# A memory-attention and expert kernel on one core: 368 steps of its hand-written order put in other places

## The chip, the cores and the metric

The kernel runs on one core of a Trainium2 chip. The metric is the device time of one execution in microseconds (us). The core has a matrix engine (PE), three engines that work along 128 partitions (DVE, ACT, POOL), and a queue engine (SP) that issues all of this kernel's transfers. The engines run side by side, each through its own instructions in order, and wait for one another by semaphores.

## The reference

```
a   = softmax(phi over the tokens)            # per batch and head: 576 tokens, 32 memories
k_m = a^T k;  v_m = a^T v                     # 32 x 64 each
att = softmax(q k_m^T / 8) v_m                # 8 batches, 8 heads, 576 tokens, 64
x   = att, heads side by side                 # 576 x 512 per batch
e   = argmax(x w_gate), kept from the token before where sigmoid(x w_local) >= 0.5
out = softmax(x w_gate)[e] * (relu(x w1[e]) w2[e])   # 8 experts, 512 -> 1024 -> 512
```

All values are 32-bit. The expert of a batch's first token is used for the whole batch; tokens that chose another are redone in a loop at the end.

## The kernel before

**Work of one batch.** The attention gives `at`, the 576 softmax rows against the memories, which are put in two terms, `ah` (ACT, L990) and `al` (POOL, L994). The product of the memories' values with `w1` (`pg`, L1220) gives `G`, again in two terms, `Gh` (ACT, L1233) and `Gl` (DVE, L1235). The hidden layer (`hidden`, L1251) multiplies these: six matmuls per group, results in a PSUM bank `ph`, and each `ph` is taken out by ACT (L1259) and DVE (L1260). Then `w2` is multiplied in two forms: `turned` (L1283 to L1285, 448 tokens) and `natural` (L1268 to L1270, 128 tokens), for which `w2` is cut into `w2h` (ACT, L1207) and `w2l` (POOL, L1208).

**What comes before that for each batch.** The tokens' maxima of `phi` (`colmax`, L699; for batch 1 a tree of four steps, `cm`, L719), their turning and spreading on PE (`pm` L736, `mc`, `pm2` L749, `cx` L758), the subtraction (`sub`, L763), the exponential (`exp`, L767), the sums over tokens (`asum`), the product with keys and values on PE (`pkv`, L794, with `sums`, L810), and the turned memories (`kvn`, `pT`, `kvT`). Then the queries are turned (`q`, `qT`), and the scores (`psc`, L925) are taken out of PSUM by DVE (`turn`, L938) and go through `mx`, `sub`, `exp`, `sum`, `inv`, `mul`, `at` (L955 to L986) in parts: `o` (one row block), `p` and `z` in batch 0, `a` and `z` in the later ones. The gate is `pl0` and `choice` (L1010, L1023 to L1025) for the first token, whose result SP reads to address `w1`, and the `g` steps for all tokens (`g pl` L1035, `g carry` L1104 to L1120, `g prob` L1127 to L1135, `g cols` L1153 to L1162).

**What sets the order.** All batches are interleaved by hand. `SCHEDULE` is a table: its line 0 runs before the first group of the first hidden layer, and line n behind the n-th piece that the generator `moe` yields. A batch yields 12 pieces of `hidden` (four of 256 tokens with two groups each, then eight of 320 tokens), 32 of `turned` and 8 of `natural`, 52 in all. So lines 1 to 52 stand beside batch 0's expert and carry mostly batch 1's attention and batch 2's keys. A step is written `2 exp 0`: batch, name. Each step appends its instructions to the engines' streams at that place, and an engine never overtakes.

**Other resources.** PSUM has three pools: `pa` (3 banks), `ph` (3), `po` (2); the table `BANKS` says which of them a step uses. All transfers are issued by SP in the order of the table, and each waits until the one eight places before it has landed. The steps `warm ...` are matmuls on zeros that are used by nobody (L694).

Of the kernel before, what the change touches and what calls it, by code (L numbers as in the profile page):

```python
# [39 lines left out]
}  # L40

SCHEDULE = """
0 warm f, 0 phi 0, 0 colmax 0, 0 phi 1, 0 colmax 1, 0 kv tile, 0 q0 tile, 0 v 0, 0 k 0, 1 kv tile, 0 at, 0 k 1, 0 warm f, 0 warm f, 0 warm b, 0 v 1, 0 pm, 0 mc, 0 pm2, 0 cx, 0 dsub 0, 0 gate constants, 0 warm f, 0 warm f, 0 warm f, 0 warm f, 0 exp 0, 0 pkv a, 0 dsub 1, 0 warm b, 0 asum 0, 0 q0 a, 0 exp 1, 0 asum 1, 0 sums, 0 rinv, 0 pkv b, 0 kvn, 0 o q, 0 pT, 0 warm b, 0 warm b, 0 q0 b, 0 gate loads, 0 q0 c, 0 kvT, 0 o psc, 0 o turn, 0 o mx, 0 o sub, 0 o exp, 0 o sum, 0 o inv, 0 o mul, 0 gate turn, 0 p q 0, 0 p q 1 0, 0 pgg, 0 o at, 0 ggt, 0 p q 1 1, 0 pl0, 0 choice, 1 phi, 0 q0 d, 1 cm 0, 1 cm 1, 1 warm k, 0 p psc, 0 p turn, 2 phi, 0 p mx, 0 p sub 0, 0 p exp 0, 0 p sub 1, 1 cm 2, 0 p exp 1, 0 p sum 0, 1 warm v, 0 p sum 1, 0 p inv, 0 p mul 1, 0 z q 0, 0 z q 1, 0 expert, 0 z q 2, 0 w1 0 a, 1 pm, 1 mc, 0 p mul 0, 0 p at 0, 0 p ah 0, 0 w1 1 a, 0 pg lo, 0 Gh lo 0, 0 z psc, 0 w2 0, 0 z turn, 1 warm u, 0 warm b, 0 p at 1, 0 z mx, 1 v, 0 p al 0, 0 pg hi, 0 p ah 1, 0 p al 1, 0 Gh lo 1, 0 Gl lo, 0 z sub, 0 G hi, 1 pm2, 1 cx, 0 pg 1 lo, 0 G 1 lo, 0 z exp, 0 z sum
1 sub 1, 0 pg 1 hi, 1 exp 1, 0 z inv, 0 z mul, 0 z at, 0 G 1 hi, 0 split 0, 1 k, 0 z ah, 1 dsub 0, 0 w2 1

0 z al, 1 exp 0, 1 asum, 0 g pl

0 split 1, 0 split 2, 0 split 3
0 g lt

2 colmax, 1 pkv 0, 1 pkv 1, 1 sums, 1 rinv, 1 q 0, 0 g L, 0 split 4
0 split 5, 0 split 6

0 split 7, 1 q 1
1 kvn, 2 pm, 2 mc, 1 a qT 0

1 z qT 0, 0 g fresh, 0 g kept  # L60

1 pT, 2 pm2

2 cx
1 kvT, 1 z qT 1, 2 sub 1, 2 sub 0, 1 a qT 1, 1 a psc, 1 pgg, 1 a turn
1 a mx, 1 a sub  # L70


1 a exp

1 a sum
2 exp 0
2 kv, 0 g carry, 0 g exp, 0 g prob, 1 a inv

# [3 lines left out]


1 ggt, 1 pl0, 2 q 0, 1 a ah, 1 a al, 2 q 1, 1 z psc, 1 choice, 2 pkv 0, 2 pkv 1, 2 sums, 0 gate 0, 1 z turn, 1 expert, 2 rinv, 1 w1 0, 1 w1 1

1 z mx
2 z qT 0, 1 z sub
2 z qT 1, 2 kvn, 2 pT, 1 pg 0, 1 w2 0, 0 gate 3, 1 z exp, 2 kvT, 0 gate 2, 1 z sum, 1 z inv, 1 z mul, 1 z at, 1 g pl, 1 g lt, 3 phi, 0 evict, 1 G 0, 2 a qT 0, 2 z psc, 1 pg 1, 1 G 1, 2 z turn, 1 split 0, 1 split 1
2 z mx
1 z ah, 1 z al, 1 split 2

0 g present, 1 w2 1
1 kv store

1 split 3, 1 split 4, 1 split 5, 3 colmax

1 split 6, 2 a qT 1, 1 split 7

1 g L  # L110

0 store, 2 a psc, 3 kv, 2 a turn, 2 pgg, 0 kv store, 3 pm, 2 a mx, 2 a sub

1 g fresh

2 a exp
1 at store

1 g kept, 2 z sub, 2 z exp, 1 g carry, 2 z sum, 2 ggt


3 q 0, 0 row store, 2 z inv, 2 z mul, 2 z at


2 a sum, 2 z ah, 2 a inv
# [6 lines left out]
3 mc
2 a at, 2 pl0, 2 choice, 2 g pl, 2 g lt, 3 pm2

3 cx


3 sub 0, 3 exp 0, 3 a qT 0, 2 a ah  # L140

1 g exp, 1 g prob
2 expert, 2 w1 0, 2 w1 1, 2 pg 0, 3 sub 1, 3 exp 1, 3 z qT 0, 3 z qT 1, 2 w2 0, 1 g cols, 1 gate 0, 1 evict, 1 gate 2, 2 a al, 3 asum, 3 pkv 0, 2 G 0, 3 pkv 1, 2 g L, 2 z al, 2 split 0, 3 sums, 3 rinv, 3 a qT 1, 2 pg 1, 1 gate 1, 2 G 1
# [2 lines left out]
2 split 1, 2 w2 1, 2 split 2  # L150
# [1511 lines left out]
```

## Time and profile before

| | |
|---|---|
| device time, median of 3 runs | 390.9 us (390.81 to 391.11) |
| the profiled execution's own time | 392.12 us |
| its span, first to last instruction | 390.3 us |
| mean granted clock of PE | 0.993 |
| busy: PE, DVE, ACT, POOL | 98%, 73%, 44%, 40% |
| DMA: bytes moved, share of the 16 engines | 82.55 MB, 70% |

The profiled execution took 392.12 us, of which 390.3 us lie between its first and last instruction and 1.8 us around them. It lies 1.2 us above the median of the runs. A busy share is a mean over the whole span; where an engine waits is seen only in the rows.

### The profile page before, as it was taken

Reading aid. Unit: us, or ns where it says so; the run is one execution under the profiler, and the core shown is the slowest. Engines: PE = TensorE matmul, PEld = TensorE weight load, DVE = VectorE, ACT = ScalarE, POOL = GpSimd, SP = SyncE. Lnnn points to the kernel's source line nnn. Section 1 sums busy time; section 2 is a strip of 40 time slices with the busy share of each in tenths; the row PEclk is TensorE's granted clock in tenths of the full one; section 3 lists DMA queues with packets and bytes.
Section 4 is the critical chain, followed back from the end, with each engine's and each line's share of the span. In section 5 each row is a group of like instructions: output and inputs, shape, how many; then the busy total and the mean of one; then the engine's idle time right before and its main releaser. Section 6 shows DMA issues by size and latency. Waiting matters only on the chain. (4 is left out here: it accounts for less than half of the span.)

```text
span 390.3 us, 10303 instructions
## 1 busy us (share of the span) xinstructions
PE 382.3 (98%) x4088; PEld 329.8 (84%) x4088; DVE 285.2 (73%) x700; ACT 170.6 (44%) x430; POOL 157.3 (40%) x166
## 2 busy tenths in 40 slices
...
GB/s 232 265 285 395 139 265 176 268 351 325 142 101 329 268 171 179 349 304 141 273 215 225 114 165 314 135 322 226 127 359 294 123 109 16 183 267 179 0 36 91
DMA packets 119947, 82.55 MB, mean 211 GB/s; under 512 B 69972, under 2 KB 95320, under 8 KB 119896
## 3 DMA queue, kind: packets, MB, share of 16 engines
...
q14 instruction: 18, 0.15, 0.1%
...
## 5 line engine op out<-in xcount | busy, mean ns | idle before, releaser
L1208 POOL TENSOR_TENSOR w2l<-raw,w2h 128x512 fp32r<-128x512 f32 x64 | 81.4, 1298 | 49.0 <-ACT w2h L1207 28.4
L1283 PE MATMUL po<-h,w2l 128*128 128x448 f32 (+1 forms) x256 | 93.3, 365 | 0.0
L1285 PE MATMUL po<-h,w2h 128*128 128x448 f32 (+1 forms) x256 | 91.8, 359 | 0.0
L1284 PE MATMUL po<-h,w2h 128*128 128x448 f32 (+1 forms) x256 | 91.8, 359 | 0.0
L1260 DVE SCALAR_TENSOR_TENSOR h<-ph,h 128x320 fp32r<-128x320 f32 (+1 forms) x96 | 52.0, 553 | 32.5 <-ACT h L1259 32.0
L1251 PE MATMUL ph<-ah,Gh 128*128 128x256 f32 (+1 forms) x256 | 73.8, 303 | 0.0
L1251 PE MATMUL ph<-ah,Gl 128*128 128x256 f32 (+1 forms) x256 | 72.2, 296 | 0.0
L1294 POOL TENSOR_TENSOR oT<-oT,gT 128x448 f32<-128x448 f32 (+1 forms) x32 | 29.1, 925 | 85.0 <-ACT gT L1160 40.7
L1259 ACT ACTIVATE h<-ph 128x320 fp32r<-128x320 f32 (+1 forms) x96 | 46.3, 489 | 29.5 <-PE ph L1251 29.3
L1251 PE MATMUL ph<-al,Gh 128*128 128x256 f32 (+1 forms) x256 | 54.9, 295 | 0.0
L1251 PEld LDWEIGHTS ph<-ah,Gh 128*128 128x128 f32 x256 | 48.2, 188 | 4.3 <-issue 1.2
L1283 PEld LDWEIGHTS po<-h,w2l 128*128 128x128 f32 x256 | 48.3, 189 | 4.1 <-issue 0.7
L1285 PEld LDWEIGHTS po<-h,w2h 128*128 128x128 f32 x256 | 48.1, 188 | 3.6
L1284 PEld LDWEIGHTS po<-h,w2h 128*128 128x128 f32 x256 | 48.1, 188 | 3.2
L1251 PEld LDWEIGHTS ph<-ah,Gl 128*128 128x128 f32 x256 | 48.3, 189 | 0.4 <-DVE Gl L1235 0.2
L994 POOL TENSOR_TENSOR al<-at,ah 128x576 fp32r<-128x576 f32 (+1 forms) x18 | 23.7, 1319 | 44.4 <-ACT ah L990 44.2
L1251 PEld LDWEIGHTS ph<-al,Gh 128*128 128x128 f32 x256 | 41.1, 188 | 0.0
L1207 ACT ACTIVATE w2h<-raw 128x512 fp32r<-128x512 f32 x64 | 37.1, 626 | 0.1
L763 POOL TENSOR_TENSOR phi_t<-phi_t,cx 128x384 f32<-128x384 f32 (+1 forms) x13 | 18.5, 1436 | 41.5 <-ACT cx L758 30.0
L965 ACT ACTIVATE sc<-sc 128x576 f32<-128x576 f32 (+2 forms) x18 | 11.3, 631 | 47.6 <-DVE sc L960 47.6
L1268 PE MATMUL po<-w2h,h 128*128 128x512 f32 (+1 forms) x80 | 29.7, 371 | 0.0
L1269 PE MATMUL po<-w2l,h 128*128 128x512 f32 (+1 forms) x80 | 29.5, 369 | 0.0
...
## 6 DMA issues: line engine op xcount, KB each, us to landing
...
```

Of the source, the lines that this page charges most:

```text
L994: (eng or nc.gpsimd).tensor_tensor(out=st.al[:, gs, ss], in0=st.at[:, gs, ss], in1=st.ah[:, gs, ss], op=ALU.subtract)
L1207: nc.scalar.activation(h, src, AF.Copy)
L1208: nc.gpsimd.tensor_tensor(out=l, in0=src, in1=h, op=ALU.subtract)
L1251: nc.tensor.matmul(pv[:, c - c0], lhsT=lt[:, g, cs], rhs=rt[:, g, s0 : s0 + n], start=(i == 0), stop=(i == 5),)
L1259: nc.scalar.activation(hi, pv, AF.Relu)
L1260: nc.vector.scalar_tensor_tensor(out=lo, in0=pv, scalar=0.0, in1=hi, op0=ALU.max, op1=ALU.subtract)
L1268: nc.tensor.matmul(po, lhsT=ht[:, c, 0, ts], rhs=hi, start=(c == 0), stop=False)
L1269: nc.tensor.matmul(po, lhsT=ht[:, c, 0, ts], rhs=lo, start=False, stop=False)
L1283: nc.tensor.matmul(po[:, 0:n], lhsT=lo, rhs=ht[:, c, 0, s1:], start=(c == 0), stop=False)
L1284: nc.tensor.matmul(po[:, 0:n], lhsT=hi, rhs=ht[:, c, 0, s1:], start=False, stop=False)
L1285: nc.tensor.matmul(po[:, 0:n], lhsT=hi, rhs=ht[:, c, 1, s1:], start=False, stop=(c == FC - 1))
L1294: nc.gpsimd.tensor_tensor(out=x, in0=x, in1=g, op=ALU.mult)
```

## The change

The first 105 lines of `SCHEDULE` (0 to 104) are written anew: the work is the same except for the matmuls on zeros, 368 steps stand in other places, and from line 105 on nothing changes. The three steps with 39, 24 and 8 small matmuls on zeros become one step with 8, `warm n`, used eight times, and there are more of the 512-column ones. For batch 0 the steps `z ah` and `z al` are cut in two. `fetch_q` makes its tile at whichever half is fetched first.

```diff
 SCHEDULE = """
...
-2 kv, 0 g carry, 0 g exp, 0 g prob, 1 a inv
...
-0 at store, 2 exp 1, 0 g cols, 0 gate 1, 1 a mul, 2 asum, 1 a at
...
-1 ggt, 1 pl0, 2 q 0, 1 a ah, 1 a al, 2 q 1, 1 z psc, 1 choice, 2 pkv 0, 2 pkv 1, 2 sums, 0 gate 0, 1 z turn, 1 expert, 2 rinv, 1 w1 0, 1 w1 1
...
+1 pl0, 0 g exp, 1 choice, 1 z mx, 1 expert, 0 g prob
...
+2 exp 0, 2 pkv 0, 2 z qT 1, 2 pkv 1, 1 z exp, 2 asum, 2 sums, 2 rinv, 1 z sum, 2 kvn, 1 w1 0, 1 w1 1, 1 pg 0, 1 pg 1, 1 z inv, 1 z mul, 1 z at, 2 pT, 1 G 0, 1 z ah, 0 gate 0, 1 z al, 1 G 1, 1 w2 0, 1 split 0, 0 gate 1, 0 gate 3
...
+3 phi, 2 z psc, 2 pgg, 1 split 3, 3 kv, 2 z turn, 0 gate 2, 0 store, 2 a psc, 2 a turn
...
     def fetch_q(st, hs):
-        if hs.start == 0:
+        if not hasattr(st, "qt"):
             st.qt = pin.tile([P, HG, NB, 32], F32, tag="q", name="q_t", bufs=1)
...
-        "idle": lambda st: [nc.sync.drain(), nc.sync.drain()],
-        "warm u": lambda st: warm(39, 32, False),
-        "warm k": lambda st: warm(24, 32, False),
-        "warm v": lambda st: warm(8, 32, False),
+        "idle": lambda st: [nc.sync.drain() for _ in range(3)],
+        "warm n": lambda st: warm(8, 32, False),
...
     for g in range(NG):
         STEPS[f"p ah {g}"] = lambda st, g=g: k_ah(st, 0, PB, each[g])
+        STEPS[f"z ah {g}"] = lambda st, g=g: k_ah(st, PB, NB, each[g])
+        STEPS[f"z al {g}"] = lambda st, g=g: k_al(st, PB, NB, gs=each[g])
```

The first removed line of the table above is old line 34, then 42 and 45; the added ones are new lines 38, 48 and 58.

PE before, at the end of line 0 and into the first hidden group (`raw` with a number is one half of `w1`'s columns, taken in two quarters; `ph<-ah,Gh` is the hidden layer):

```order
L694 MATMUL wp<-wz 128x512
L1220 MATMUL pg<-raw_461,kvT 32x256 x8
L749 MATMUL pm<-ident,mcw 128x128
L1220 MATMUL pg<-raw_473,kvT 32x256 x8
L1251 MATMUL ph<-ah,Gh 128x256
L1251 MATMUL ph<-ah,Gl 128x256
```

PE in the changed kernel, at the same place:

```order
L1220 MATMUL pg<-raw_518,kvT 32x256 x8
L1251 MATMUL ph<-ah,Gh 128x256
L1251 MATMUL ph<-ah,Gl 128x256
L1251 MATMUL ph<-ah,Gh 128x256
L1251 MATMUL ph<-ah,Gl 128x256
L1251 MATMUL ph<-al,Gh 128x256 x2
L1251 MATMUL ph<-ah,Gh 128x256
L1251 MATMUL ph<-ah,Gl 128x256
L1251 MATMUL ph<-ah,Gh 128x256
L1251 MATMUL ph<-ah,Gl 128x256
L1251 MATMUL ph<-al,Gh 128x256 x2
L1220 MATMUL pg<-raw_521,kvT 32x256 x8
```

The product with the third quarter of `w1`'s columns (`pg<-raw_473`, eight matmuls, the step `0 pg 1 lo`) stood ahead of the hidden layer; it now stands, as `pg<-raw_521`, behind the first two hidden groups. `pm2` (L749) has moved further forward, and two matmuls on zeros and batch 0's `z psc` stand ahead of the piece shown.

ACT before, beside batch 0's `turned` and `natural` (`phi_t` is batch 2's exponential, `gT` and `gt` batch 0's gate values, `kvn` batch 2's):

```order
L767 ACTIVATE phi_t<-phi_t 128x4x192
L1075 ACTIVATE ex<-ex 32x144
L1125 ACTIVATE pr<-rt 32x18
L767 ACTIVATE phi_t<-phi_t 128x4x96
L1160 ACTIVATE gT<-gs 32x14 x4
L1162 ACTIVATE gt<-gs 32x1 x4
L876 ACTIVATE ggt_113<-pgg 128x9 x2
L990 ACTIVATE ah<-at 128x2x288
L832 ACTIVATE kvn<-pkv,rinv 128x128 x2
```

ACT in the changed kernel:

```order
L1075 ACTIVATE ex<-ex 32x144
L1125 ACTIVATE pr<-rt 32x18
L767 ACTIVATE phi_t<-phi_t 128x4x96
L990 ACTIVATE ah<-at 128x2x288
L1160 ACTIVATE gT<-gs 32x14 x4
L1162 ACTIVATE gt<-gs 32x1 x4
L767 ACTIVATE phi_t<-phi_t 128x4x192
L965 ACTIVATE sc<-sc 128x576
L832 ACTIVATE kvn<-pkv,rinv 128x128 x2
```

The larger exponential of batch 2 (128x4x192) stood ahead of the gate's eight copies; it now stands behind them, and directly ahead of the work that `pkv` releases.

## Rows read from the trace of the kernel before

**Rows 1.** The page's head and its first part: span, busy us and share of PE.
```profile
span 390.3 us, 10303 instructions
PE 382.3 (98%) x4088; PEld 329.8 (84%) x4088; DVE 285.2 (73%) x700; ACT 170.6 (44%) x430; POOL 157.3 (40%) x166
```

**Rows 2.** Windows: us; busy PE, PEld, DVE, ACT, POOL; granted clock; DMA share; GB/s.
```profile
26.00:28.00 2.00, 2.00 (x66) 1.28 (x47) 1.97 (x7) 1.02 (x3) 0.23 (x1) 0.68 0.92 306
28.00:30.00 2.00, 2.00 (x26) 0.75 (x33) 2.00 (x5) 1.19 (x4) 1.35 (x2) 0.50 1.02 345
34.00:44.00 10.00, 10.00 (x229) 9.40 (x228) 7.96 (x15) 7.97 (x18) 8.92 (x9) 1.00 0.98 286
```

**Rows 3.** Timeline of PE: start, us, instruction, count, idle before and its releaser.
```profile
19.35 0.77 PE L694 MATMUL wp<-wz 128*128 128x32 bf16 x24
20.05 0.66 PE L925 MATMUL psc<-qT,kvT 64*32 64x256 f32 x16
...
20.94 1.97 PE L912 MATMUL pq<-ident,q 128*64 128x128 f32 x32
...
24.73 0.30 PE L736 MATMUL pm<-ident,cm 128*128 128x128 f32 x1 [1.46 <-DVE cm L719]
25.01 1.01 PE L1220 MATMUL pg<-raw,kvT 64*32 64x256 f32 x9
...
26.65 1.64 PE L694 MATMUL wp<-wz 128*128 128x32 bf16 x40
28.22 1.23 PE L1220 MATMUL pg<-raw,kvT 64*32 64x256 f32 x16
...
29.79 0.79 PE L1220 MATMUL pg<-raw,kvT 64*32 64x256 f32 x16
30.50 0.39 PE L1251 MATMUL ph<-ah,Gh 128*128 128x256 f32 x1
...
32.13 0.66 PE L1220 MATMUL pg<-raw,kvT 64*32 64x256 f32 x16
```

**Rows 4.** Timelines of ACT, DVE and SP's queue, 18 to 24 us.
```profile
18.60 0.25 ACT L876 ACTIVATE ggt<-pgg 128x9 f32<-128x9 f32 x2
19.09 0.63 ACT L914 ACTIVATE qT<-pq 128x512 f32<-128x512 f32 x1 [0.24 <-PE pq L912]
...
19.73 0.15 DVE L1024 FIND_INDEX8 ei<-m,pl 1x8 uint32<-1x8 f32 x1
...
20.70 0.69 DVE L719 TENSOR_TENSOR tree<-phi_t 128x512 f32<-128x512 f32 x1 [0.56 <-DMA phi_t<-in_phi_dram]
...
20.61 3.25 SPq L1185 DMA_DIRECT2D raw<-in_moe_w_dram  x4
```

**Rows 5.** Timeline of PE beside batch 0's turned and natural products.
```profile
56.50 0.71 PE L925 MATMUL psc<-qT,kvT 64*32 64x288 f32 x16
...
69.70 2.21 PE L794 MATMUL pkv<-kv_t,phi_t 64*32 64x128 f32 x143
```

**Rows 6.** Timeline of DVE, 57 to 68 us.
```profile
57.30 0.85 DVE L938 STREAM_TRANSPOSE sc<-psc 128x288 f32<-128x288 f32 x2 [2.53 <-PE pgg L866]
58.18 0.75 DVE L955 TENSOR_REDUCE mx<-sc 128x18 f32<-128x576 f32 x1
...
61.15 0.22 DVE L1104 STREAM_TRANSPOSE endt<-end 32x64 f32<-32x64 f32 x1
...
62.27 0.25 DVE L1127 TENSOR_REDUCE es<-ex 32x18 f32<-32x144 f32 x1
...
64.83 0.18 DVE L1153 SCALAR_TENSOR_TENSOR gs<-pr,rb 32x18 f32<-32x18 f32 x1
...
65.60 2.24 DVE L699 TENSOR_REDUCE asum<-phi_t 128x128 f32<-128x1152 f32 x1
```

**Rows 7.** Timeline of ACT, 60 to 67 us.
```profile
60.35 0.83 ACT L767 ACTIVATE phi_t<-phi_t 128x768 f32<-128x768 f32 x1
...
65.04 0.89 ACT L1160 ACTIVATE gT<-gs 32x14 f32<-32x14 f32 x4 [2.04 <-DVE gs L1153]
65.96 0.84 ACT L1162 ACTIVATE gt<-gs 32x1 f32<-32x1 f32 x4
```

More of the change, by code (lines that the diff above doesn't have):

```diff
@@ L42 @@
 SCHEDULE = """
-0 warm f, 0 phi 0, 0 colmax 0, 0 phi 1, 0 colmax 1, 0 kv tile, 0 q0 tile, 0 v 0, 0 k 0, 1 kv tile, 0 at, 0 k 1, 0 warm f, 0 warm f, 0 warm b, 0 v 1, 0 pm, 0 mc, 0 pm2, 0 cx, 0 dsub 0, 0 gate constants, 0 warm f, 0 warm f, 0 warm f, 0 warm f, 0 exp 0, 0 pkv a, 0 dsub 1, 0 warm b, 0 asum 0, 0 q0 a, 0 exp 1, 0 asum 1, 0 sums, 0 rinv, 0 pkv b, 0 kvn, 0 o q, 0 pT, 0 warm b, 0 warm b, 0 q0 b, 0 gate loads, 0 q0 c, 0 kvT, 0 o psc, 0 o turn, 0 o mx, 0 o sub, 0 o exp, 0 o sum, 0 o inv, 0 o mul, 0 gate turn, 0 p q 0, 0 p q 1 0, 0 pgg, 0 o at, 0 ggt, 0 p q 1 1, 0 pl0, 0 choice, 1 phi, 0 q0 d, 1 cm 0, 1 cm 1, 1 warm k, 0 p psc, 0 p turn, 2 phi, 0 p mx, 0 p sub 0, 0 p exp 0, 0 p sub 1, 1 cm 2, 0 p exp 1, 0 p sum 0, 1 warm v, 0 p sum 1, 0 p inv, 0 p mul 1, 0 z q 0, 0 z q 1, 0 expert, 0 z q 2, 0 w1 0 a, 1 pm, 1 mc, 0 p mul 0, 0 p at 0, 0 p ah 0, 0 w1 1 a, 0 pg lo, 0 Gh lo 0, 0 z psc, 0 w2 0, 0 z turn, 1 warm u, 0 warm b, 0 p at 1, 0 z mx, 1 v, 0 p al 0, 0 pg hi, 0 p ah 1, 0 p al 1, 0 Gh lo 1, 0 Gl lo, 0 z sub, 0 G hi, 1 pm2, 1 cx, 0 pg 1 lo, 0 G 1 lo, 0 z exp, 0 z sum
@@ L44 @@
[L44 to L76, printed above, removed]
-2 kv, 0 g carry, 0 g exp, 0 g prob, 1 a inv
@@ L85 @@
-0 at store, 2 exp 1, 0 g cols, 0 gate 1, 1 a mul, 2 asum, 1 a at
-1 ggt, 1 pl0, 2 q 0, 1 a ah, 1 a al, 2 q 1, 1 z psc, 1 choice, 2 pkv 0, 2 pkv 1, 2 sums, 0 gate 0, 1 z turn, 1 expert, 2 rinv, 1 w1 0, 1 w1 1
[L93 to L127, printed above, removed]
+0 warm f, 0 phi 0, 0 colmax 0, 0 phi 1, 0 colmax 1, 0 kv tile, 0 q0 tile, 0 v 0, 0 k 0, 1 kv tile, 0 at, 0 k 1, 0 warm f, 0 warm f, 0 warm b, 0 v 1, 0 pm, 0 mc, 0 pm2, 0 cx, 0 dsub 0, 0 gate constants, 0 warm f, 0 warm f, 0 warm f, 0 warm f, 0 exp 0, 0 pkv a, 0 dsub 1, 0 warm b, 0 asum 0, 0 q0 a, 0 exp 1, 0 asum 1, 0 sums, 0 rinv, 0 pkv b, 0 kvn, 0 o q, 0 pT, 0 warm b, 0 warm b, 0 q0 b, 0 gate loads, 0 kvT, 0 o psc, 0 o turn, 0 o mx, 0 o sub, 0 o exp, 0 o sum, 0 p q 1 0, 0 o inv, 0 o mul, 0 gate turn, 0 o at, 1 phi, 1 cm 0, 0 p q 0, 0 pgg, 1 cm 1, 0 q0 c, 0 p q 1 1, 0 q0 d, 0 warm n, 0 warm n, 0 ggt, 0 pl0, 0 choice, 1 cm 2, 0 warm n, 0 warm n, 0 p psc, 0 p turn, 0 p mx, 0 p sub 0, 0 p exp 0, 0 warm n, 0 warm n, 0 warm n, 0 warm n, 0 warm b, 0 warm b, 0 warm b, 0 warm b, 0 p sub 1, 0 p exp 1, 1 pm, 1 mc, 0 p sum 0, 0 p sum 1, 1 k, 0 z q 0, 0 z q 1, 0 z q 2, 0 expert, 1 pm2, 0 p inv, 0 p mul 0, 1 cx, 0 p mul 1, 0 p at 0, 0 p ah 0, 0 warm b, 0 p al 0, 0 p at 1, 0 p ah 1, 0 p al 1, 0 warm b, 0 warm b, 1 dsub 0, 0 warm b, 0 w1 0 a, 0 w1 1 a, 0 pg lo, 0 Gh lo 0, 0 Gh lo 1, 0 Gl lo, 0 warm b, 0 warm b, 1 v, 0 z psc, 0 z turn, 0 z mx, 0 pg hi, 0 G hi, 0 z sub, 1 exp 0
@@ new lines @@
+0 pg 1 lo, 0 G 1 lo, 0 z exp, 0 z sum
+0 pg 1 hi, 0 G 1 hi, 0 z inv, 0 z mul, 0 z at, 1 sub 1, 1 exp 1, 1 asum, 0 z ah 0, 2 phi, 2 colmax
+1 pkv 0, 1 pkv 1, 1 sums, 1 rinv, 0 z al 0, 0 z ah 1, 0 g pl, 0 z al 1, 0 w2 0, 0 split 0, 0 split 1, 0 split 2, 0 split 3, 2 pm
+0 w2 1, 0 split 4, 1 q 0
+1 q 1
+0 split 5, 0 split 6, 2 mc
+1 kvn
+0 at store
+0 split 7
+2 kv, 0 g lt, 0 g L, 0 g fresh
+1 a qT 0, 1 pT, 1 z qT 0
+1 kvT
+1 z qT 1
+1 a qT 1
+1 pgg, 1 ggt, 2 q 1, 0 g kept, 0 g carry, 1 a psc, 1 a turn, 1 a mx, 1 a sub, 1 z psc, 2 pm2, 2 cx
@@ new lines @@
+1 a exp, 1 a sum, 1 a inv, 1 a mul, 1 a at
+2 sub 0
+1 z turn
+1 pl0, 0 g exp, 1 choice, 1 z mx, 1 expert, 0 g prob
+2 sub 1, 2 exp 1
+1 a ah, 1 z sub, 0 g cols
+1 a al
+2 exp 0, 2 pkv 0, 2 z qT 1, 2 pkv 1, 1 z exp, 2 asum, 2 sums, 2 rinv, 1 z sum, 2 kvn, 1 w1 0, 1 w1 1, 1 pg 0, 1 pg 1, 1 z inv, 1 z mul, 1 z at, 2 pT, 1 G 0, 1 z ah, 0 gate 0, 1 z al, 1 G 1, 1 w2 0, 1 split 0, 0 gate 1, 0 gate 3
+2 q 0, 2 kvT, 1 split 1, 0 evict
+1 split 2, 1 w2 1, 2 z qT 0, 2 a qT 0
+2 a qT 1
+3 phi, 2 z psc, 2 pgg, 1 split 3, 3 kv, 2 z turn, 0 gate 2, 0 store, 2 a psc, 2 a turn
@@ L129 @@
+2 ggt, 2 z mx
+2 z sub
+1 split 4, 1 split 5
+1 split 6, 1 split 7
+0 row store
+3 colmax, 2 a mx, 2 a sub, 1 g pl, 2 a exp, 3 pm, 2 a sum, 0 g present, 2 a inv
+2 z exp, 2 z sum
 3 q 1
+2 z inv, 1 at store
 2 a mul
[L134 to L147, printed above, removed]
+1 g lt, 1 g L, 1 g fresh, 1 g kept
```

6 lines of the change are left out of this document (added).

## The prediction

> **What bounds the kernel now.** I read the busy shares first: PE is busy for 382.3 of 390.3 us [rows 1], so a change of order can give back only what PE loses, and that has to be found by place. [...] Third, the timeline of PE up to the first hidden group: `pm` waits 1.46 us for DVE's `cm` at 24.73, the clock falls some two us behind that pause, and the first hidden matmul runs at 30.50 [rows 3]. What the reader is to take from it: all the time to be won lies ahead of 30.50. Behind it every moved step can only keep PE fed as now, or starve it.
>
> **The head (line 0).** In the changed order the fillers and `z`'s queries stand where PE paused, `pm2` and the queries stand ahead of `w1`'s products, and the third quarter's product `pg 1 lo` has left the head. I lay PE's work end to end. `ggt` is now behind the second `qT` copy, which ended at 19.09 + 0.63 = 19.72, and takes 0.25 [rows 4], so `pl0` starts at 20.0. Then, at durations of rows 3: `pl0` 0.2 (an estimate, it is four short matmuls); 16 fillers at 0.77 / 24 = 0.032, 0.5; `p psc` 0.6; 32 fillers, 1.0; four of 512 columns; `pm` 0.3; `z`'s queries 2.3 (from 20.94 to where the pause began, 24.73 - 1.46 = 23.27); `pm2` 0.3; four of 512; `pg lo` 0.66; two of 512; `z psc` 0.5 (`psc` at 56.50, 0.71 with its tail [rows 5]); `pg hi` 0.66. A 512-column filler costs at most twice a 256-column step: twelve of those and their tail stand between 30.50 and 32.13, 0.136 each, so 0.27; ten make 2.7. That adds up to 20.0 + 9.7 = 29.7; as 0.136 holds the change of shape too, I take 29.4. The product at full clock is the row at 32.13 (0.66), not those at the lower level (1.23, and 0.79 across its end). So the hidden layer starts 1.1 us earlier, but `pg 1 lo`, 0.66, now comes out of it: **a gain of 0.45**.
>
> Two covers can fail here. The choice of the expert comes later, since `pl0` and two steps of the tree (0.69 and some 0.4) are ahead of it on DVE: it ended near 19.9 and will end near 21.0 [rows 4], so the first load of `w1` is issued at 21.6, not at 20.61. Before, its first quarter was used 25.01 - 20.61 = 4.4 us after the issue; that makes 26.0. Ahead of it in the queue now stand 1152 KB of keys, where 576 KB of `phi` stood; at the 345 GB/s of rows 2 the difference is 1.7 us if no idle room takes it up, so 26.0 to 27.7, and PE wants it at 27.1. Bounds for the head: from +0.2 (load 0.6 late) to -0.95 (512-column steps at less than 0.24 us, so a start at 28.9).
>
> A 32-column filler costs 0.032 us in the row above [rows 3]. [...]
>
> **Line 48, the new wait.** Before, batch 2's larger exponential ran at 60.35 [rows 7] and its sum over tokens at 65.60 to 67.84 [rows 6], while `pkv` used them at 69.70 [rows 5]: 8.5 us and 1.9 us to spare. Now the exponential stands on ACT behind the gate's eight copies, and these wait for DVE's `gs`, which stands behind nearly all of batch 1's first attention part and the start of the second.
> - When PE wants it: `pkv` has moved from line 45 to line 48, three natural pieces of three 512-column matmuls, 9 x 0.23 to 0.27; with 0.45 gained, 69.70 + 2.1 - 0.45 = 71.3.
> - When it is ready: `a turn` starts at 57.6 (57.30, one turned piece of 0.6 and `pgg` 0.15 later, 0.45 earlier). From there to the end of `gs` took 65.01 - 57.30 = 7.7 us [rows 6]. The carry, 62.27 - 61.15 = 1.1, now stands ahead of it and drops out; `mul`, `at`, and `z`'s `turn`, `mx` and `sub` come in, five at 0.75 [rows 6], 3.7, and the choice, four small ones, 0.6. So `gs` ends near 57.6 + 10.9 = 68.5. The copies take 65.96 + 0.84 - 65.04 = 1.8, the exponential 0.83 [rows 7]: 71.1.
> - 71.1 against 71.3 is a draw if nothing on DVE waits. But `turned`'s copy out of PSUM and `pl0` stand in between and each waits for PE; these can put it 0.8 later. I take 0.3.
> - `asum` (2.24) can start only then, while `pkv` takes 2.0 (71.7 - 69.70): the one-column matmuls behind `pkv` wait another 0.3.
> Behind the waiting `pkv` on PE stand `w1`'s products of batch 1, `pT` and the rest of `natural`, so all of PE moves. Together **0.6 lost**; bounds 0 and 0.9 + 0.4 = 1.3.
>
> **Line 58.** Batch 2's `a psc` takes two of the three `ph` banks in the middle of batch 1's hidden layer. Before, it stood in `turned`, where nothing else uses them. The banks come free with `a turn`, which stands behind `z turn` on DVE; each takes 0.85 [rows 6]. Counted from the hidden group ahead of them, the second group behind wants a bank after `z psc`, `pgg`, `a psc` and one group, 0.5 + 0.2 + 0.5 + 0.9 = 2.1 us; `z turn` can start at 0.7, after the group's own eviction at about 1.1, and the first bank is out after 1.1 + 0.85 + 0.43 = 2.4. **0.3 lost**; bounds 0 and 0.8 (if DVE is late by one more step of its size, and never less, as no work goes).
>
> **The rest.** I cost the finer `z ah` and `z al`, the eight `split`s of batch 0, and `fetch_q` at nothing: they stand beside a hidden layer and a `turned` on which PE now waits for no one [rows 2]. The splits' engine POOL was the fullest there (8.92 of 10 us), so if its cover goes the price is of the size of line 48's. The same holds for batch 2's load of `w1`, whose choice now stands behind the gate's products. Bounds 0 and 0.6.
>
> **Sum.** -0.45 + 0.6 + 0.3 = +0.45. The profiled execution would go from 392.12 us (390.3 of span and 1.8 around it) to 392.6. It was 1.2 above the median of its runs, so I put the difference on the median: 390.9 + 0.45 = **391.4 us**. That is below what a measurement of this kernel can tell from no change, 0.2% or 0.8 us.
>
> **The rivals.**
> 1. *Faster: the head wins and the waits are covered.* The new waits are sums of DVE steps with errors of some tenths, and line 48 is a draw. With the head between -0.45 and -0.95 and nothing lost, 390.45 to 389.95; I write 390.1. For it: PE now waits nowhere behind 34 us. Against it: two stretches with spare time of 8.5 and 1.9 us go to about zero.
> 2. *Slower: line 48's chain decides.* If `gs` comes at 69.4 or later, PE waits the full 1.3 there, and with `ph` at 0.8: -0.45 + 1.3 + 0.8 = +1.65, 392.5. It decides once `gs` ends more than 0.2 us behind 68.5, for then each tenth on DVE is a tenth on PE. For it: an engine never overtakes, and eight ACT copies stand between `gs` and the exponential. Against it: DVE can have idle time that I counted as work.
> 3. *Slower: the clock falls again.* It fell behind a pause and a run of short fillers [rows 2, 3]; the new head has no pause but more fillers. [...]
>
> **How the numbers follow.** Forecast (no measurable change, 391.4; own range 390.7 to 391.9) 0.47; rival 1 0.18; rival 2 0.26; rival 3 0.09. Of the forecast 0.06 lies above 391.7; of rival 1 about 0.12 lies below 390.1 and 0.06 above. So faster 0.12, no change 0.41 + 0.06 = 0.47, slower 0.06 + 0.26 + 0.09 = 0.41. The range 390.2 to 393.0 leaves out a tenth at either end.
>
> **What the profile after would show.** The head is right if the first hidden matmul starts between 28.9 and 29.7, at clock 1.00 in the windows from 20 to 34 us, with `pg 1 lo` at about 0.66 behind two groups. Line 48 is right if `pkv` shows an idle time of some tenths released by ACT's exponential (L767), and the one-column matmuls (L810) one released by DVE's `asum` (L699). Line 58 is right if one hidden group in batch 1 waits some tenths for DVE's `turn` (L938). From 130 us on the two timelines should run in parallel, shifted by the sum. I am wrong if PE waits in batch 0's `turned` for `w2l`, if batch 1's or 2's `pg` waits for its load, or if the head begins above 30.

## The result and the profile after

The changed kernel takes 394.14 us (median of 6 runs, 393.76 to 395.49) against 391.0 of the kernel before beside it: a ratio of 1.0076, 95% interval 1.006 to 1.0093, so some 3.0 us slower. Predicted were 391.4 us and a range of 390.2 to 393.0; the time lies above it.

The page's head and its first part, of the changed kernel:

```profile
span 392.0 us, 10300 instructions
PE 383.0 (98%) x4086; PEld 329.4 (84%) x4090; DVE 290.7 (74%) x700; ACT 170.7 (44%) x431; POOL 157.9 (40%) x166
```

Against [rows 1] PE's work is nearly the same, but DVE is busy 5.5 us longer with the same 700 instructions: some of them take longer. That row holds the first clue, and nothing in the order of the instructions shows it. The windows, as in [rows 2]:

```profile
26.00:28.00 2.00, 1.84 (x50) 0.78 (x50) 1.74 (x5) 1.22 (x4) 1.69 (x2) 1.00 1.07 345
28.00:30.00 2.00, 2.00 (x36) 1.65 (x28) 1.97 (x5) 1.45 (x4) 1.31 (x2) 1.00 1.06 381
34.00:44.00 10.00, 9.41 (x221) 8.67 (x221) 8.45 (x15) 5.91 (x13) 8.76 (x10) 1.00 0.93 241
```

The clock stays at 1.00 in the head, and now PE idles between 34 and 44 us, where before it did not. PE's timeline in the head, as in [rows 3]:

```profile
22.42 0.27 PE L736 MATMUL pm<-ident,cm 128*128 128x128 f32 x1
...
24.88 0.33 PE L749 MATMUL pm<-ident,mcw 128*128 128x128 f32 x1
...
26.00 0.66 PE L1220 MATMUL pg<-raw,kvT 64*32 64x256 f32 x16
...
27.13 0.72 PE L925 MATMUL psc<-qT,kvT 64*32 64x288 f32 x16
...
28.21 0.39 PE L1251 MATMUL ph<-ah,Gh 128*128 128x256 f32 x1
...
29.84 0.66 PE L1220 MATMUL pg<-raw,kvT 64*32 64x256 f32 x16
```

The pause before `pm` is gone and the first hidden matmul runs at 28.21, where [rows 3] have 30.50. The moved product stands behind two groups and takes its 0.66. PE's waits over the whole span (us in total, times, longest):

```profile
PE pkv L810 <- DVE asum L699: 0.8, 1, 0.8
PE pkv L794 <- ACT phi_t L767: 0.7, 1, 0.7
...
PE pkv L794 <- issue: 0.3, 1, 0.3
...
PE pm L736 <- DVE cm L699: 0.3, 1, 0.3
```

The body, from the first hidden matmul to PE's last work, took 355.96 us before and takes 359.82 now. The ends of matmuls are modelled, so I place the loss by start-to-start times instead: each gap between two matmuls of PE, less the time of one product of that width. Those that are new and over 0.25 us:

```
start of gap   between                              beyond the product   what PE waited for
 37.17         batch 1's pkv, 29 records in          0.51                 "issue"
 39.06         pl (batch 0) and pm (batch 2)         0.49                 DVE's column max of batch 2
 71.03         natural and batch 2's pkv (line 48)   0.86                 ACT's larger exponential
 74.10         batch 2's pkv and its sums            0.27                 DVE's asum
124.12         batch 3's pkv and its sums            0.95                 DVE's asum
```

They make 3.08; with the moved product (0.66) that is 3.74 of the body's 3.86. From 130 us on the two kernels run in parallel, as predicted, but on the wrong side.

**Line 48.** DVE, POOL, ACT and PE there, answering to [rows 5 to 7]:

```profile
58.89 1.91 DVE L960 TENSOR_TENSOR sc<-sc,mx 128x576 f32<-128x576 f32 x1
...
62.85 0.76 DVE L982 TENSOR_TENSOR sc<-sc,sm 128x576 f32<-128x576 f32 x1
...
69.19 0.22 DVE L1153 SCALAR_TENSOR_TENSOR gs<-pr,rb 32x18 f32<-32x18 f32 x1
...
58.34 3.33 POOL L763 TENSOR_TENSOR phi_t<-phi_t,cx 128x768 f32<-128x768 f32 x2 [8.20 <-ACT cx L758]
...
69.44 0.89 ACT L1160 ACTIVATE gT<-gs 32x14 f32<-32x14 f32 x4 [4.25 <-DVE gs L1153]
...
71.22 0.84 ACT L767 ACTIVATE phi_t<-phi_t 128x768 f32<-128x768 f32 x1
...
72.12 2.25 PE L794 MATMUL pkv<-kv_t,phi_t 64*32 64x128 f32 x144 [0.70 <-ACT phi_t L767]
```

The chain is the one predicted: `gs`, eight copies, the exponential, `pkv`. But `gs` ends at 69.41 and not at 68.5, and 1.15 of that is one instruction: a DVE subtraction that takes 0.76 elsewhere takes 1.91 while POOL subtracts too. **Batch 3's sums**, where I had predicted nothing, show the same twice over:

```profile
114.81 1.68 DVE L1105 TENSOR_TENSOR_SCAN cr<-endt 1x18 f32<-1x18 f32 x1
...
116.76 0.71 DVE L1116 SCALAR_TENSOR_TENSOR es<-sc,crt 32x32 f32<-32x32 f32 x1
...
117.92 0.92 DVE L1128 TENSOR_SCALAR es<-es 32x18 f32<-32x18 f32 x1
...
120.25 0.22 DVE L1153 SCALAR_TENSOR_TENSOR gs<-pr,rb 32x18 f32<-32x18 f32 x1
...
122.85 2.24 DVE L699 TENSOR_REDUCE asum<-phi_t 128x128 f32<-128x1152 f32 x1 [0.23 <-ACT phi_t L767]
...
114.60 2.82 POOL L763 TENSOR_TENSOR phi_t<-phi_t,cx 128x768 f32<-128x768 f32 x2
117.38 1.43 POOL L994 TENSOR_TENSOR al<-at,ah 128x576 fp32r<-128x576 f32 x1
...
122.29 0.52 ACT L767 ACTIVATE phi_t<-phi_t 128x384 f32<-128x384 f32 x1
...
125.14 0.27 PE L810 MATMUL pkv<-ones,asum 64*32 64x1 f32 x16 [0.75 <-DVE asum L699]
```

The scan of 18 values (0.18 elsewhere) takes 1.68 and ends at 116.49, when the first of POOL's two subtractions is over (114.60 to 116.44); the small `L1128` (0.17 elsewhere) ends at 118.84, with POOL's `al`. `gs` comes 2.7 us late, and behind it the gate's eight copies, the exponential, the sums and PE. In the first 140 us seven DVE instructions are stretched like this, before none. Behind 140 us, where the order is the same, both traces have six rows stretched by 0.3 us or more. So the trace of the kernel before shows the effect too, only later than the rows that I read:

```profile
238.87 1.39 DVE L960 TENSOR_TENSOR sc<-sc,mx 128x576 f32<-128x576 f32 x1
...
237.80 3.34 POOL L763 TENSOR_TENSOR phi_t<-phi_t,cx 128x768 f32<-128x768 f32 x2 [5.77 <-ACT cx L758]
```

Reductions, transposes and instructions that read PSUM are not stretched in this trace: no 128x576 reduction (L955) takes over 0.76 us, no 128x576 transpose (L893, L986) over 0.79 and no 128x512 `Gl` (L1235, which reads `pg` in PSUM) over 0.71, though many of them run while POOL does. Both sorts stand side by side at 98 us:

```profile
97.53 0.74 DVE L955 TENSOR_REDUCE mx<-sc 128x18 f32<-128x576 f32 x1
98.31 1.13 DVE L960 TENSOR_TENSOR sc<-sc,mx 128x576 f32<-128x576 f32 x1
...
96.27 2.55 POOL L1208 TENSOR_TENSOR w2l<-raw,w2h 128x512 fp32r<-128x512 f32 x2
```

### The profile page after: what moved, and what is told of

The parts are those of the page before. It is cut to its first block, busy times and chain, and to the rows that moved or that the text cites. A ratio compares the mean times of both kernels' runs of the same rounds, so it can differ in the third digit from the quotient of the medians.

```text
span 392.0 us, 10300 instructions
## 1 busy us (share of the span) xinstructions
PE 383.0 (98%) x4086; PEld 329.4 (84%) x4090; DVE 290.7 (74%) x700; ACT 170.7 (44%) x431; POOL 157.9 (40%) x166
## 5 line engine op out<-in xcount | busy, mean ns | idle before, releaser
L763 POOL TENSOR_TENSOR phi_t<-phi_t,cx 128x384 f32<-128x384 f32 (+1 forms) x13 | 19.1, 1476 | 29.4 <-ACT cx L758 17.8
L1268 PE MATMUL po<-w2h,h 128*128 128x512 f32 (+1 forms) x80 | 29.7, 371 | 0.0
L1270 PE MATMUL po<-w2h,h 128*128 128x512 f32 (+1 forms) x80 | 29.5, 369 | 0.0
```

Source lines behind the costliest of these rows:

```text
L1268: nc.tensor.matmul(po, lhsT=ht[:, c, 0, ts], rhs=hi, start=(c == 0), stop=False)
L1270: nc.tensor.matmul(po, lhsT=ht[:, c, 1, ts], rhs=hi, start=False, stop=(c == FC - 1))
```

## The experiments

A ratio is to the kernel before, run beside it on the same chip, with its 95% interval. One and the same kernel's runs spread by 0.6 to 3.1 us (in `abcn` by more), and in the eight traces of kernels with the changed line 0 the first hidden matmul starts between 28.17 and 30.28 (29.1 in the mean), partly by how long PE waits for the first keys (1.1 us in `a_sub_early`, 0.3 in `d_pkv_late`), and in four of them behind an "issue" stop near 24 us (0.24 to 1.3). So single terms are read from gaps and bodies, and times only where they differ by more.

**The kernel before once more.**

> The kernel before, unchanged. Its profiled execution had a fall of the clock (mean 0.993, 3.3 us at the lower level) and took 392.12 us against a median of 390.9. If that fall is not in most executions, the executions at clock 1.00 take about 390.9 and their profile shows the first hidden matmul near 29.3 instead of 30.50; the head of the changed kernel (28.21) is then worth 1.1 minus the moved product 0.66, about 0.4, and not 1.6. If the fall is in every execution, the clock is 0.993 again and the first hidden matmul stands at 30.5.

1.0003 [0.9988, 1.0018]. Its profile has no fall of the clock (0.999), the first hidden matmul at 29.54 and the body at 355.94. So the fall in [rows 2] is not in every execution: against one without it the changed head starts 1.33 earlier, not 2.29. It is no single case either. Of the 72 runs of the kernel before in the experiments, 27 have a mean granted clock of 0.993 to 0.997 and take 392.1 us (median); the other 45 take 391.1. Of the 48 runs with the changed line 0, one has. So the new head does keep the clock, as the prediction had it; where in a run the clock fell is known only where there is a trace. The bodies agree to 0.02 us, so a body's difference of 0.2 means something.

**One wait at a time.** Three kernels, each the changed one with a few steps moved:

```diff
 a_sub_early (new line 18)
+2 pm2, 2 cx, 2 sub 0, 2 sub 1
 o_exp_early (new line 41; it leaves line 48)
+2 exp 0
 c_sub3_early (new lines 77 and 79)
+3 mc
+3 pm2, 3 cx, 3 sub 0, 3 sub 1
```

> The changed kernel; pm2, cx and both subtractions of batch 2's phi on POOL are moved from lines 27, 36 and 41 to line 18, so that POOL is through with them before DVE's scores of batch 1 (pm2 in bank ph). [...] Queue theory (the exponential's place behind the gate's eight copies alone makes the wait): the wait stays at 0.5 or more, gain under 0.4.

> The changed kernel; only batch 2's larger exponential is moved from line 48 to line 41, ahead of the gate's eight copies. DVE's sub at 58.89 still meets POOL and takes 1.9. [...] If the time stays, the wait was covered by something else.

> The changed kernel; for batch 3 mc goes from line 93 to 77, and pm2, cx and both subtractions on POOL from lines 93 and 103 to 79, so that POOL is idle while DVE does the carry and prob of batch 1. The exponentials stay where they are, the second behind the gate's eight copies. [...] Queue theory: the wait stays above 0.5.

I took the stretch of DVE beside POOL for the cause. From the first kernel I expected the subtraction at 58.89 back at 0.76, the waits of 0.86 and 0.27 at 0 to 0.2, and 1.0 to 1.1 us, 393.0; from the second no wait of `pkv` for the exponential, and the same time; from the third the rows of 1.68, 0.71 and 0.92 back at 0.18, 0.24 and 0.17, the wait of 0.95 gone, and 0.9 to 1.0 us, 393.2.

With batch 2's POOL subtractions at line 18, DVE and POOL read:

```profile
60.61 0.76 DVE L960 TENSOR_TENSOR sc<-sc,mx 128x576 f32<-128x576 f32 x1
...
52.83 2.83 POOL L763 TENSOR_TENSOR phi_t<-phi_t,cx 128x768 f32<-128x768 f32 x2 [1.12 <-ACT cx L758]
```

Both are short again, and the gap at `pkv` goes from 0.86 to 0; the body loses 0.78. The gap ahead of the sums stays (0.23 for 0.27). The exponential moved alone clears both. With batch 3's subtractions early the gap of 0.95 is gone. These waits are thereby tied to their causes. Yet the ratios are 1.0079 [1.0048, 1.0111], 1.0067 [1.0048, 1.0086] and 1.0068 [1.0037, 1.0098]: no gain to speak of. In each trace the gap released by "issue" grew or a new one came: in batch 1's `pkv` 0.74, 1.18 and 0.73 for 0.51, and 0.71 in batch 2's hidden layer in the third.

**All three waits out, and the "issue" gap.** `abc` takes the two subtraction moves and `2 pm` from line 4 to line 7.

> The changed kernel with three waits taken out: batch 2's second max, constants and both subtractions issued at line 18 and batch 3's at line 79 in place of behind the earlier batch's z scores, and batch 2's max transposes from line 4 to line 7. Theory (VectorE instructions that stand while GpSimd's running one ends make TensorE wait 0.49 for batch 2's column max, 0.86 + 0.27 at batch 2's token sums and 0.95 at batch 3's): all four gone, first hidden product to last TensorE work 359.8 -> 357.3 to 357.9, time 391.6 to 392.2; the 0.66 of the moved gate product and the load gap in batch 1's token sums (0.5 to 1.2) stay. Rival (the lost time is spread over the order in the expert phases and the waits only show it): body 359 or more, time 393.5 or more.

1.0065 [1.0039, 1.009], 393.25 us. The gaps of 0.49, 0.86 and 0.95 are gone (that of 0.27 stays), and the body is 359.68: **the rival's number, though not its reason**. The lines of PE that differ from the changed kernel are `pl` and `pm` -0.35, `natural` ahead of `pkv` -0.77, batch 3's `pkv` -1.04; and the other way batch 1's `pkv` +0.94, one hidden phase at 227 us +0.53, products with `w1` +0.18 and the first hidden phase +0.11. So 2.16 was won and 1.76 lost; the body is only 0.14 shorter, and the other 0.26 is not placed. Batch 1's `pkv` in that kernel:

```profile
36.23 1.34 PE L794 MATMUL pkv<-kv_t,phi_t 64*32 64x128 f32 x72
38.83 0.80 PE L794 MATMUL pkv<-kv_t,phi_t 64*32 64x128 f32 x38 [1.25 <-issue]
```

PE stops inside one group of equal matmuls, with its operands there. The page's DMA part has a queue for instructions, whose transfers keep step with PE's records:

```profile
q8 instruction: 33, 0.54, 0.6%
```

These are 33 transfers of 16 KB for 8251 records of PE (matmuls, weight loads, and 75 of its sequencer), 250 each. I counted the records ahead of each stop, and took the start of the last such transfer ahead of it:

```
kernel         stops (us)        records ahead   modulo 256   transfer began   from its start to PE's restart
after          37.17 -> 37.75    1214            190          35.37            2.38
abc            37.31 -> 38.83    1214            190          36.36            2.47
abc            227.30 -> 227.88  5310            190          225.41           2.47
n_shift        80.09 -> 81.98    2238            190          79.30            2.68
n_shift        131.25 -> 132.03  3262            190          129.67           2.36
n_shift        230.08 -> 232.57  5309            189          230.08           2.49
before_shift   126.03 -> 126.83  3262            190          124.54           2.29
before_shift   224.66 -> 226.79  5311            191          224.52           2.27
```

In the twenty traces 24 stops of over 0.25 us are released by "issue". All of them stand within five records of the same place modulo 256 (some traces hold four more early records than others), and end 2.3 to 2.8 us behind the start of a 16 KB transfer. So I take it that PE waits for its own next block of instructions, one block to a transfer: 256 records fit all the stops, and 250 to a transfer is near that. A `pkv` burst is about 318 records in 2.2 us, so it runs through more than a block in less time than the 2.3 to 2.8 us that PE waits from the start of a transfer.

**Moving the blocks and nothing else.** The changed kernel, the kernel without the waits, and the kernel before, each with idle matmuls near the start in another mix, 44 records more ahead of all that follows:

```diff
 n_shift, abcn (line 0)
-0 k 1, 0 warm f, 0 warm f
+0 k 1, 0 warm n, 0 warm n, 0 warm n, 0 warm n, 0 warm n
-0 p exp 0, 0 warm n, 0 warm n, 0 warm n, 0 warm n
+0 p exp 0, 0 warm n, 0 warm n, 0 warm b, 0 warm b
 before_shift (old line 0)
-0 k 1, 0 warm f, 0 warm f
+0 k 1, 1 warm v, 1 warm v, 1 warm v
```

> The changed kernel with other idle products ahead of the first expert phase: the two 512-column ones behind the first k product become five 32-column groups, and two of the later 32-column groups become two 128-column ones, so that TensorE has some 48 more instructions ahead of batch 1's token sums and nothing else moves. Theory (TensorE stops in that burst where the block of 256 of its instructions that it has reached is not yet loaded: 0.5 to 1.2 us before the record of index 1218 in all four traces so far): the boundary now falls some 48 records further ahead, among longer products, the gap of 0.51 inside the burst is gone, and the time is 0.5 to 0.8 below the changed kernel's (393.3 to 393.8). Rival (the gap there is a late operand, a transfer or a semaphore of the token sums): a gap of 0.4 to 1.2 stays inside the burst, wherever the index falls, and the time is the changed kernel's 394.1. A stall elsewhere of the same 0.5 would be for the first theory with no gain in time.

> The kernel with the three waits taken out and also the other idle products in the head, which move the boundary of TensorE's instruction blocks away from batch 1's token sums. Theory: waits and block load together are the whole loss beside the moved 0.66: body 356.6 to 357.2, time 391.0 to 391.6, that is no slower than before. Rival (block loads only move to another burst, 0.5 to 0.8 each): body as without the other idle products, 357.3 to 358, time 391.6 to 392.2.

> The kernel before with its order as it is, and only two idle 512-column products near the start replaced by 24 idle 32-column ones, as close to the same TensorE time as they come: all that follows has some 44 more TensorE records ahead of it. Theory (TensorE stalls where a block of 256 of its instructions passes faster than the next one is loaded; in every trace so far the stalls stand at record index 189 to 191 modulo 256): from the record times of before, blocks would end behind the bursts of token sums near 43.7, 124, 222 and 322 us, the body (first hidden product to last work) grows by 3 to 7 us at stalls that stand at that same index, time 394 to 399. Rival (the 8 us that the other idle products cost the changed kernel came from the clock or from its steps): body within 0.5 of 355.95, time within 1 us of before.

`n_shift` takes 402.25 us, 1.0289 [1.0265, 1.0313]. The gap in batch 1's `pkv` is gone as the theory has it, but four new ones have come at its index (three in the table, and 1.21 at record 702 in the head): my time, 393.3 to 393.8, was wrong by more than 8 us since I had not asked where the other boundaries would fall. `abcn`, 402.7 us, 1.0314 [1.0271, 1.0356], lost as much; 391.0 to 391.6 was expected. Then I did ask, from the record times of before, and `before_shift` takes 397.08 us, 1.0127 [1.0102, 1.0151], inside the 394 to 399 on record, its body 4.48 longer. Of the four places named for its stops, three have one, at 45.5 (0.40), 126.0 (0.68) and 224.7 (1.98); near 322 there is none. PE's timeline and the windows at its costliest stop:

```profile
224.66 0.41 PE L1251 MATMUL ph<-ah,Gh 128*128 128x320 f32 x1
226.79 0.41 PE L1251 MATMUL ph<-ah,Gl 128*128 128x320 f32 x1 [1.72 <-issue]
...
228.46 0.47 PE L1251 MATMUL ph<-ah,Gh 128*128 128x320 f32 x1
```
```profile
224.00:227.00 3.00, 1.28 (x69) 1.04 (x50) 1.33 (x7) 1.06 (x3) 3.00 (x3) 1.00 0.87 227
227.00:230.00 3.00, 3.00 (x13) 3.00 (x13) 1.18 (x2) 1.19 (x3) 2.36 (x3) 0.54 0.78 202
```

The stop costs twice: 1.98 by itself, and behind it the clock falls (0.54 in the second row) and matmuls of 0.31 take 0.47. So the kernel before, with not one step in another place, can be made 5 us slower by the count of its idle matmuls. The changed kernel has nearly its count, so this is not the whole of its loss; but of the 1.76 that `abc` lost again, 1.47 is the growth of two such stops.

**What stands behind the moved sums.** To take batch 1's `pkv` away from the load I put it two lines later in `abc`, as before has it; two more kernels change one thing in that.

```diff
 d_pkv_late (abc, from line 4 to line 6)
+1 pkv 0, 1 pkv 1, 1 sums, 1 rinv, 0 w2 1, 0 split 4, 1 q 0
 dm (d_pkv_late, line 0)
-0 warm n
+0 warm b, 0 warm b, 0 warm b, 0 warm b, 0 warm b, 0 warm b
 d_pg_head (d_pkv_late, end of line 0; they leave line 1)
+0 pg 1 lo, 0 G 1 lo
```

> The kernel with the three waits taken out, and batch 1's token sums two lines later, at line 6, among the hidden products as in the kernel before. Theory (the 1.45 gap in these sums is the block load that started at 36.4 and ended at 38.8; two lines later it is loaded): gap gone, body 359.7 -> 358.0 to 358.5, time 391.5 to 392.1 against 393.25. Rival (the gap is a late operand or the burst itself): a gap of over 0.7 goes with the sums and the time stays at 393.

> As the kernel with the token sums later, with one group of idle 32-column products in the head replaced by six of 512 columns: 4 records fewer ahead of all that follows. Theory: the block boundary near 227 us, which stalled 0.42 in a hidden phase, falls 4 records later and stalls under 0.15, nothing else moves by more than 0.3; time 0 to 0.5 lower than without it. Rival (the place of the boundary does not matter by single records): the same 0.42 there.

> As the kernel with the token sums later, with the first half of batch 0's second gate product and its split back ahead of the first hidden product, as before. The prediction's term: first hidden product 0.45 to 0.7 later, body 0.66 shorter, so the time within 0.3 of the kernel without this edit. Rival (the gate product ran in the head under other waits): first hidden product no later, time 0.5 to 0.7 lower.

```profile
36.71 0.46 PE L1035 MATMUL pl<-at,ggt 128*32 128x160 f32 x2
38.53 0.73 PE L1035 MATMUL pl<-at,ggt 128*32 128x160 f32 x14 [1.36 <-DVE at L986]
...
40.31 0.41 PE L1251 MATMUL ph<-ah,Gh 128*128 128x320 f32 x1 [0.56 <-ACT ah L990]
```

In `d_pkv_late` the gap is gone, and PE waits 1.58 and 0.72 (start to start) for batch 0's `z` scores, which the sums had covered: 395.94 us, 1.010 [1.0074, 1.0126], where 391.5 to 392.1 was expected. `dm` (1.0126 [1.0101, 1.015]) tells nothing: the stall it was to shift is not in `d_pkv_late`, and its clock falls behind the `z` wait (0.70 from 40 to 44 us). `d_pg_head` (1.0129 [1.01, 1.0159]) is inconclusive: the product in the head waits 1.0 for its load of `w1`, so the first hidden matmul is 1.22 later for a body 0.44 longer.

**What the head's early start is worth.** `head_only` has the new line 0 and before's order from there (the gate's third quarter behind the first hidden group, as the new head needs it).

> The changed kernel's head alone (the first gate product behind the first hidden product, the changed order of the keys, scores and first z steps ahead of it), and from line 1 on the order of before. Theory (the head starts the expert phases 0.9 to 1.3 earlier than a run of before without the clock's fall, at 28.2 to 28.7 against 29.5, and pays 0.66 for the moved product; all of the rest of the loss lies in the later steps): body 356.0 + 0.66 = 356.6, time 390.3 to 391.1 against 391.1 to 391.8 of before. Rival (the earlier start is given back because the chain of batch 1's scores behind it is no earlier): a wait of 0.5 or more at batch 1's token sums or at line 4 to 6, and the time within 0.3 of before or above it.

1.0071 [1.0047, 1.0095], the rival: the first hidden matmul at 29.30, and 1.68, 0.46 and 0.61 lost at 35 to 41 us, again for batch 0's `z`. I thought its product stood too late, and moved it:

```diff
 after_z, abc_z, d_z, head_z (line 0)
-0 p al 1, 0 warm b, 0 warm b, 1 dsub 0, 0 warm b
+0 p al 1, 0 z psc, 0 z turn, 0 warm b
-1 v, 0 z psc, 0 z turn, 0 z mx
+1 v, 0 warm b, 0 warm b, 0 z mx, 1 dsub 0
```

> The changed kernel with batch 0's z scores product and its turn moved ahead of the first gate product (1.6 us earlier, near 25.5, in the place of two idle products, which take its old place; batch 1's first subtraction on VectorE goes behind z's max). [...] Rival (z was late because VectorE was full, not because of its product): z's last transpose within 0.5 of 37.48, time as the changed kernel's.

> The kernel with the three waits taken out, with z's scores early as well. Theory: its remaining loss is the block load in batch 1's token sums (1.45), which the early z does not touch: body 359.7 -> 359.2 to 359.7, time 392.7 to 393.3. Rival (the token sums stood in z's shadow and the gap hid it): body 358.5 or less, time under 392.3.

> The kernel with the token sums two lines later, with z's scores early. Theory (what took the gain of the later sums was the wait of 1.58 and 0.72 for z's scores, which had stood behind the sums): both under 0.5, body 360.8 -> 358.2 to 359.0, time 393.2 to 394.2 against 395.9. Rival (these waits come from the later order of lines 2 to 6): waits over 1.5 stay in sum.

> The changed head alone, with z's scores early and before's order from line 1 on. Theory (the head alone lost at the wait of 1.68, 0.46 and 0.61 for z's scores and their split): in sum under 0.9, body 359.7 -> 357.0 to 358.0, time 391.3 to 392.3 against 394.06; then the early start pays its 0.66 and ties with before. Rival (the z wait is not the scores' place): over 1.8 of these waits stays, time over 393.

That theory fell. In `after_z` the last transpose of `z` was to end 1.3 to 2 us ahead of 37.48, and the time to be 393.4 to 393.9. Ratios 1.0096 [1.0077, 1.0116], 1.0055 [1.0036, 1.0074], 1.0142 [1.012, 1.0164] and 1.009 [1.0072, 1.0108]; the last transpose of `z` ends at 38.39 in `after_z` and 37.48 in the changed kernel, 9.3 us behind the first hidden matmul in both (before: 5.0), and the waits stay. (`abc_z`'s body is 1.06 shorter than `abc`'s; 0.65 of that is the "issue" gap in batch 1's `pkv`, 0.80 for 1.45.) `z` advances between other work on DVE, and the order there differs in one step: before, `0 G 1 hi` stands behind `0 z at`, now ahead of `0 z inv`. So two more:

```diff
 d_g (d_pkv_late, line 2)
-0 pg 1 hi, 0 G 1 hi, 0 z inv, 0 z mul, 0 z at
+0 pg 1 hi, 0 z inv, 0 z mul, 0 z at, 0 G 1 hi
 head_d (head_z, line 2; 1 dsub 0 and 1 exp 0 leave line 0)
+0 z at, 0 z ah, 0 split 0, 1 dsub 0, 0 w2 1
```

> The kernel with batch 1's token sums two lines later (and the three waits out), with one step moved: the split of the last gate quarter (0 G 1 hi, two VectorE halves of 0.37) stands behind z's last transpose in line 2, as before, in place of ahead of z's reciprocal. Theory (VectorE is full from 28 to 38 us, and the order of its steps there, not the place of z's product on TensorE, makes z late): z's last transpose ends 0.7 to 2 us earlier (it also gets ahead of GpSimd's tree), the waits of 1.58 and 0.72 for it fall to under 0.6 in sum, but the hidden products of the last quarter now wait 0.5 to 1.4 for that split; time 0 to 1.5 below 395.94. Rival (z is late because the first hidden group is early, whatever the order): waits over 1.8 in sum stay.

> The changed head alone with z's scores early, and two steps put back where before has them: batch 1's subtraction on VectorE (0.95) and its larger exponential behind z's last transpose, and batch 0's first weight split on ScalarE behind z's ah. Theory (VectorE is full there): z's last transpose ends 0.9 earlier (37.3 -> 36.4), the waits of 1.67, 0.43 and 0.61 fall to 0.5 to 1.0 in sum, time 392.8 to 393.6 against 394.82. Rival: waits over 1.8 in sum stay and the time is within 0.4 of 394.8.

In `d_g` the waits for `z` are gone, `z` is done 7.3 us behind the first hidden matmul instead of 9.3, and PE waits instead for the split that was moved:

```profile
37.91 0.39 PE L1251 MATMUL ph<-ah,Gl 128*128 128x256 f32 x1 [1.37 <-DVE Gl L1235]
```

1.53 start to start; 394.95 us, 1.0075 [1.0061, 1.009]. What made `z` earlier is seen on DVE, in `d_pkv_late` (the first two lines) and in `d_g`:

```profile
35.06 1.22 DVE L976 TENSOR_SCALAR sm<-sm 128x18 f32<-128x18 f32 x1
...
36.61 1.05 DVE L982 TENSOR_TENSOR sc<-sc,sm 128x576 f32<-128x576 f32 x1
...
35.47 0.17 DVE L976 TENSOR_SCALAR sm<-sm 128x18 f32<-128x18 f32 x1
...
35.97 0.76 DVE L982 TENSOR_TENSOR sc<-sc,sm 128x576 f32<-128x576 f32 x1
```

Of the 2.0 us, 0.67 is the split that no longer stands ahead of `z`. The other 1.34 is POOL again: in `d_pkv_late` its tree of batch 1's sums runs from 34.95 and stretches these two steps; in `d_g` it starts at 36.03, behind the start of both, and its own first step takes 1.83 for 1.29. `head_only`, `head_z` and `head_d`, with no tree there, have 7.9. `head_d` missed: 0.95 us less DVE work ahead of `z` left it there, since DVE then idled for the evictions and `Gl`s it stands between (1.0093 [1.0075, 1.0111]). So of the 4.2 us by which `z` is later than before, the stretch beside POOL makes 1.34 and the split of the last quarter of `w1` 0.67; the other 2.2 (7.27 for 5.04) no run took apart. In these orders DVE either splits late, and PE waits 1.5, or finishes `z` late, and PE waits 2.3 unless another batch's sums fill the hole, as the changed order has it. A tree that starts later on POOL, with the split ahead of `z`, was not run.

None of the changed kernels beats the kernel before; the best, `abc_z` and `abc`, are 0.55% and 0.65% behind it.

## Why the prediction was wrong

Point by point, against the profile of before without the clock's fall:

- **The head**: predicted -0.45, measured 29.54 to 28.21 less the product, -0.67. That the two are close is luck. I counted the gain from 30.50, a start 0.96 later than the one without the clock's fall, and put it on a median of runs most of which have no fall: from 29.54 my start of 29.4 would have made a loss of 0.5. And 28.21 is the second earliest of the eight traces with that line 0 (28.17 to 30.28; three lie within my 28.9 to 29.7, one above 30, my sign of being wrong). With their mean, 29.1, the head costs some 0.2.
- **Line 48**: predicted 0.6 (0 to 1.3), measured 0.86 + 0.27 = 1.13. The mechanism and both releasers were right; the size was off by the stretch of one subtraction, which took 1.91 where my sum has 0.76.
- **Line 58**: predicted 0.3, measured nothing: the step from `psc` to `ph` at 88.52 has 0.20 beyond the product, the same as at 182.71, where the order is old.
- **"The rest", costed at nothing with bounds 0 and 0.6: the step that failed.** It measured 1.95: 0.95 at batch 3's sums, 0.49 at batch 2's `pm` and 0.51 in batch 1's `pkv`, none of which it names. I argued that these steps stand beside work on which PE waits for no one, and took every DVE duration from rows in which POOL was elsewhere. The sentence looked at POOL only as an engine that might be full, not as one beside which a DVE instruction takes 1.68 for 0.18; and of PE's own instruction loads the prediction has no term.
- **Rival 2** had the direction and one of the places (392.5): line 48 cost 1.13 of its 1.3, line 58 nothing of its 0.8. Rival 3 did not come: the clock is at 1.00. That a fall is in some executions and not in others, the 72 runs of the kernel before now show (27 and 45). The range's upper end, 393.0, takes in a fall that costs the changed kernel's work 1.65 us, my estimate; no run shows that term, and between the kernel before's runs with a fall and those without lie 1.0 us (392.1 and 391.1).

Sum: -0.67 + 1.13 + 0.95 + 0.49 + 0.51 = +2.41; the two traces differ by 388.03 - 385.48 = 2.55 at PE's last work. With the mean start of the eight traces in place of 28.21 the sum is +3.3, beside 3.1 between the medians; that is an estimate. Shown by undoing: the waits at batch 2's and batch 3's `pkv` and their sums, and what causes each. Argued only: the cause of the 0.49, for `abc` moved the `pm` that waits and not what it waits for; the rows have 1.33 of stretch on DVE ahead of it (`z`'s two steps at 34.06 and 35.61 take 1.21 and 1.05). Shown by moving blocks: the cause of the "issue" stop. Seen in the traces: that such stops grow when data waits go. No kernel here has all of these waits out at once, so that their sum is the whole loss rests on the gaps and not on a time. Not settled: why a block's load starts 203 records ahead of the stop in one row of the table, 120 in another and 1 to 33 in the rest, which decides how long PE stands; and the last 0.1 to 0.3 us of the body.
